# Two small touch loads (44 packets in all) ahead of the first full loads of an attention and gMLP kernel

## The chip, the cores and the metric

One core of a Trainium2 chip runs the whole program. The metric is device time in microseconds (us); lower is better. A run's time is some 1.2 us longer than the span that a profile shows of it. A granted TensorE clock that is halved for a few microseconds shows as a mean clock of 0.998 instead of 1.0.

## The reference, cut to what matters

```python
h = x + _A_ref(_layernorm(x), wq, wk, wv, wo, beta)       # 32 heads, 4 segments of 512 rows, with a memory
return h + _B_ref(_layernorm(h), w_in, w_sp, b_sp, w_out) # gated MLP
```

x is 2048 x 1024 in bf16, and wv is 1024 x 1024 (2 MB). The first thing that TensorE can do is v = layernorm(x) @ wv for the first 512 rows. It needs x by chunks of 128 rows and wv by blocks of 128 rows. Such a block of wv (256 KB) is called a wv row below.

## The kernel before

Every operation is recorded by a helper and then put in order for each engine by a static scheduler; the order of TensorE is fixed by the program. All loads are issued by SyncE. Start of the program, with cuts (the comments on the right are added here):

```python
N_WARM = 11
LOAD = "1 0:1 1:3 2 3:4 4:5 3 5:6 6:8"          # x chunk 1, wv row 0, wv rows 1-2, x chunk 2, ...
START = ("t00 t01 u00 u01 v00 u02 v01 T10 T11 v02 u03 v03 u10 ...")   # TensorE's order
...
ZERO = tens("zero", [128, L], BF16, R_E + 2048)
for k in range(N_WARM):
    mm(PS[:, 7, :], ZERO[:, 0:128], ZERO[:], True, True)
...
for h in range(2):
    x_cols(0, h)                                 # x chunk 0, two halves
for c in LOAD.split():
    if ":" in c:
        wv_rows(*map(int, c.split(":")))
    else:
        dma(XIN[int(c)][:], x2d[int(c) * 128:int(c) * 128 + 128, :])
act(G1[:, 0:1], ZERO[:, 0:1], ACTF.Sqrt)         # loads the first activation table
```

In START, t and T are transposes of a chunk of x. u and v are the two halves of the wv product, with the chunk as the first digit and the wv row as the second. So u01 is the first matmul that needs "1:3", the 512 KB load of wv rows 1 and 2. The text calls it the critical load; the prediction writes "wv rows 1 to 3" for it, after the slice.

The softmax here doesn't subtract the row's maximum and nothing guards it: scores larger than these inputs give would overflow.

Of the kernel before, what the change touches and what calls it, by code (L numbers as in the profile page):

```python
# [7 lines left out]
BF16 = mybir.dt.bfloat16  # L8
# [18 lines left out]
PE, ACT, DVE, POOL, SP = range(5)  # L27
# [319 lines left out]
def bass_sequential_preLN__memory_aug_infini_attn__mixer_gmlp__prompt_kernel(  # L347
# [14 lines left out]
    x2d = A_x[0]  # L362
# [9 lines left out]
    def region(size):  # L372
        a = cur[0]
        cur[0] += (size + 31) // 32 * 32
        assert cur[0] <= ARENA, cur[0]
        return a

    def tens(name, shape, dt, off=None):
        sz = int(np.prod(shape[1:])) * mybir.dt.size(dt)
        if off is None:  # L380
            off = region(sz)
        assert off % 32 == 0 and off + sz <= ARENA, (name, off, sz)
        t = nc.alloc_sbuf_tensor_at(name, list(shape), dt, offset=abase + off)
        G.base[t.name] = off
        return t
# [15 lines left out]
    R_E = region(20480)  # L401
# [52 lines left out]
    def n_of(ap):  # L454
        return int(np.prod([x[1] for x in list(ap.ap)[1:]]))

    def inps(ap):
        return ap.tensor.name == PS.name
# [15 lines left out]
    def act(o, i, func, scale=1.0, prio=0, bias=None):  # L474
        r = [i] + [x for x in (scale, bias) if x is not None and not isinstance(x, float)]
        kw = {} if bias is None else {"bias": bias}
        G.op(ACT, lambda e: e.activation(o, i, func, scale=scale, **kw), r, [o],  # L477
             ((172 if inps(i) else 224) + n_of(i)) / 1.2 + 26, prio=prio, name=str(func))
# [39 lines left out]
    def dma(o, i, transpose=False, after=False, eng=SP):  # L518
        nb = n_of(o) * list(o.ap)[0][1] * mybir.dt.size(o.dtype)
        d = G.op(eng, lambda e: e.dma_start(o, i, transpose=transpose), [i], [o], 1230.0 if transpose else 400.0, dma=True,  # L520
             nbytes=nb * (2.1 if transpose else 0.92 if n_of(o) == D or o.tensor.name == WV.name else 1.0), name=("T:" if transpose else "D:") + o.tensor.name)
        if after:
            d.deps.add(G.last_pe)
# [4 lines left out]
    def bank():  # L528
        b = bank_set[0][bank_rr[0] % len(bank_set[0])]
        bank_rr[0] += 1  # L530
        return PS[:, b, :]
# [9 lines left out]
    def wv_rows(a, b):  # L541
        dma(WV[:, a:b, :], A_wv.rearrange("(c p) n -> p c n", p=128)[:, a:b, :])
# [7 lines left out]
    for c in LOAD.split():  # L550
        if ":" in c:
            wv_rows(*map(int, c.split(":")))
        else:
            dma(XIN[int(c)][:], x2d[int(c) * 128:int(c) * 128 + 128, :])
    act(G1[:, 0:1], ZERO[:, 0:1], ACTF.Sqrt)
    iot = tens("iot", [128, 128], I32, R_E)
    G.op(POOL, lambda e: e.iota(iot[:], [[1, 128]], base=0, channel_multiplier=-1), [], [iot[:]], 400)
# [264 lines left out]
    for x in START.split():  # L822
        c, i = int(x[1]), int(x[2])
# [5 lines left out]
        b = PS[:, 2 + 2 * (c % 3) + h, :]  # L829
# [12 lines left out]
    for lo, hi in ((0, 128), (128, 512)):  # L842
        b = bank()
# [83 lines left out]
    for pair in range(16):  # L927
        a, b = 2 * pair, 2 * pair + 1
# [213 lines left out]
```

## Time and profile before

| | before |
|---|---|
| median of 3 runs | 794.76 us (794.14 to 795.21) |
| the profiled run | 796.87 us, span 795.6, mean clock 0.998 |
| critical load, issue to landing | 5.92 us, landed at 8.57 |
| start of u01 | 8.61 us |

### The profile page before, as it was taken

What the parts mean: (1) busy time and instruction counts of PE and PEld (TensorE: products, weight loads), DVE (VectorE), ACT (ScalarE), POOL (GpSimd) and SP (SyncE); (2) the same over time, 40 slices, a digit from 0 to 9 for tenths busy, and PEclk for the clock granted to TensorE, in tenths of its full rate; (3) what the DMA queues carried; (4) which work ended last, traced back from release to release, by engine and by line L of the source; (5) the groups of instructions that cost most, each with busy time, mean ns of one, the idle gap of its engine ahead of it and who ended that gap; (6) DMA issues with size and microseconds to landing.
All of it is one profiled execution on the core that took longest, in us unless ns stands there. A gap on an engine that the chain in (4) does not pass through costs nothing.

```text
span 795.6 us, 12064 instructions
## 1 busy us (share of the span) xinstructions
PE 790.3 (99%) x5369; PEld 321.2 (40%) x4760; DVE 369.9 (46%) x854; ACT 293.0 (37%) x351; POOL 138.8 (17%) x269
## 2 busy tenths in 40 slices
PE   8999999999999999999999999999999999999999
PEld 2455554555554542341322414443244334424433
DVE  6784687878775686804215042132233222322222
ACT  5788887787768862133323323100000000000000
POOL 1354544444433331200001010000000000000000
PEclk9999999999999999999999999999999999999999
DMA  7676812742234648510000016703410530012001
GB/s 245 179 167 140 173 42 67 138 90 55 68 75 112 159 115 228 159 42 1 0 1 1 20 34 148 202 1 64 121 34 1 119 100 1 0 54 61 0 1 53
DMA packets 128550, 65.02 MB, mean 82 GB/s; under 512 B 96624, under 2 KB 119408, under 8 KB 128496
## 3 DMA queue, kind: packets, MB, share of 16 engines
q1 hardware_dynamic: 128496, 64.25, 33.2%
q8 instruction: 39, 0.64, 0.4%
q14 instruction: 15, 0.12, 0.1%
HBM read 32.51 MB, written 8.39 MB: 51 GB/s over the span
## 4 chain that ended last, share of the span: by engine, by line
PE 98%; DMA 1%; ACT 0%; SPq 0%; issue 0%; DVE 0%
PE ps L327 80%; PE ps L328 15%; PE ps L468 3%; DMA wv<-in_A_wv_dram 1%; ACT e L477 0%; SPq L520 0%; PE ps L472 0%; DVE hx L499 0%
## 5 line engine op out<-in xcount | busy, mean ns | idle before, releaser
L327 PE MATMUL ps<-wspT,z 128*128 128x512 bf16 x896 | 194.0, 379 | 0.0
L477 ACT ACTIVATE e<-ps 128x2048 bf16<-128x2048 f32 x80 | 149.8, 1873 | 35.1 <-PE ps L468 35.1
L327 PEld LDWEIGHTS ps<-wspT,z 128*128 128x128 bf16 x896 | 87.7, 98 | 106.4 <-issue 1.0
L477 ACT ACTIVATE z<-ps 128x512 bf16<-128x512 f32 x120 | 63.1, 571 | 145.4 <-PE ps L327 145.4
L499 DVE TENSOR_TENSOR tg<-ps,brow 128x512 bf16<-128x512 f32 x56 | 38.7, 691 | 150.0 <-PE ps L327 122.0
L327 PE MATMUL ps<-hnT,win 128*128 128x512 bf16 x448 | 97.3, 379 | 0.0
L718 POOL TENSOR_SCALAR_AFFINE_SELECT e<-e 128x1024 bf16<-128x1024 bf16 (+1 forms) x80 | 77.1, 963 | 113.9 <-ACT e L477 113.6
L328 PE MATMUL ps<-win,hnT 128*128 128x512 bf16 (+1 forms) x384 | 90.1, 344 | 0.0
L327 PE MATMUL ps<-wout,y 128*128 128x512 bf16 (+2 forms) x252 | 85.8, 367 | 0.0
L572 DVE BATCH_NORM_STATS2 stats<-z 128x6 f32<-128x448 bf16 x64 | 40.1, 627 | 97.0 <-ACT z L477 95.4
L328 PE MATMUL ps<-wout,y 128*128 128x512 bf16 x210 | 79.6, 379 | 0.0
L499 DVE TENSOR_TENSOR hx<-hx,ps 128x512 bf16<-128x512 bf16 (+1 forms) x65 | 42.3, 675 | 77.3 <-PE ps L327 76.9
L327 PEld LDWEIGHTS ps<-hnT,win 128*128 128x128 bf16 x448 | 43.8, 98 | 54.2 <-issue 2.0
L327 PE MATMUL ps<-wv,xnT 128*128 128x512 bf16 x251 | 60.7, 384 | 1.6 <-DMA wv<-in_A_wv_dram 1.1
L327 PE MATMUL ps<-xnT,wk 128*128 128x512 bf16 (+2 forms) x264 | 60.8, 374 | 0.0
L327 PE MATMUL ps<-xnT,wq 128*128 128x512 bf16 x256 | 60.8, 380 | 0.0
L327 PE MATMUL ps<-wo,oT 128*128 128x512 bf16 x256 | 58.8, 379 | 0.0
L327 PEld LDWEIGHTS ps<-wout,y 128*128 128x128 bf16 x252 | 24.2, 98 | 72.2 <-issue 69.1
L327 PE MATMUL ps<-win,hnT 128*128 128x512 bf16 x128 | 48.5, 379 | 0.0
L327 PEld LDWEIGHTS ps<-win,hnT 128*128 128x128 bf16 x128 | 12.5, 98 | 81.4 <-issue 80.9
L513 POOL TENSOR_SCALAR rs<-mv 128x1 f32<-128x1 f32 x44 | 11.0, 250 | 194.2 <-DVE mv L575 194.2
L327 PEld LDWEIGHTS ps<-v,e 128*128 128x128 bf16 x1280 | 40.1, 96 | 9.8 <-issue 1.7
(76 smaller groups left out, 640.0 us busy)
## 6 DMA issues: line engine op xcount, KB each, us to landing
win<-in_B_w_in_dram SPq DMA_DIRECT2D x6, 1024.0 KB, 5.8
hx<-in_A_x_dram SPq DMA_DIRECT2D x16, 256.0 KB, 3.3
out_dram<-hx SPq DMA_DIRECT2D x16, 256.0 KB, 2.4
hx<-out_dram SPq DMA_DIRECT2D x16, 256.0 KB, 2.7
out_dram<-hx SPq DMA_DIRECT2D x31, 128.0 KB, 1.7
xin<-in_A_x_dram SPq DMA_DIRECT2D x15, 256.0 KB, 4.9
wout<-in_B_w_out_dram SPq DMA_DIRECT2D x2, 1792.0 KB, 11.0
wq<-in_A_wq_dram SPq DMA_DIRECT2D x2, 1024.0 KB, 7.9
```

Of the source, the lines that this page charges most:

```text
L327: return e.matmul(out, lhsT, rhs, start=start, stop=stop)
L328: return e.add_instruction(mybir.InstMatmult(name="I-%d" % (1000000 + o.idx), engine=e.engine, ins=[e.lower_ap(rhs), e.lower_ap(lhsT)], ou ...
L468: G.op(PE, lambda e: e.matmul(o, lhsT, rhs, start=True, stop=True, tile_position=(32 * i, 0)), [lhsT, rhs], [o], n / 2.4 if last else 3.5, ...
L477: G.op(ACT, lambda e: e.activation(o, i, func, scale=scale, **kw), r, [o], ((172 if inps(i) else 224) + n_of(i)) / 1.2 + 26, prio=prio, na ...
L499: G.op(DVE, lambda e: e.tensor_tensor(o, a, b, op), [a, b], [o], vcost(o, [a, b], fast), name="tt", prio=late[0])
L513: G.op(POOL, lambda e: e.tensor_single_scalar(o, i, s, op), [i], [o], 220 if n_of(o) < 8 else 220 + 2.5 * n_of(o), name="pts1", prio=late[0])
L572: G.op(DVE, lambda e, si=si, so=so: e.bn_stats(so, si), [si], [so], (cs + 143) / 0.96, name="bn_stats", prio=late[0])
L718: G.op(POOL, lambda e: e.affine_select(d, d, pat, ALU.is_ge, 0.0, base=0, channel_multiplier=-1), [d], [d], 1270 if j else 640, name="mask")
```

## The change

The intent: if the first read of each 64 KB piece of memory costs extra, a tiny read of every piece ahead of the full loads should pay for it early. The two touches go through ScalarE's queue, so that they delay none of SyncE's issues.

```diff
+    touch = [tens("touch%d" % i, [32, 32], BF16, R_E + 4096 + 64 * i) for i in range(2)]
+    dma(touch[0][:], A_wv.rearrange("(a b) n -> a b n", b=32)[:, 0, 0:32], eng=ACT)
+    dma(touch[1][0:12, :], x2d[128:512, :].rearrange("(a b) n -> a b n", b=32)[:, 0, 0:32], eng=ACT)
     act(G1[:, 0:1], ZERO[:, 0:1], ACTF.Sqrt)
```

## The prediction

> **What bounds the kernel now.** I read the page first: the busy shares, the slices, the chain that ended last. Then, because the change touches only the first loads, I read the first 26 us: the chain of waits in that stretch, TensorE's timeline, and a table by windows.
>
> ```profile
> PE 790.3 (99%) x5369; PEld 321.2 (40%) x4760; DVE 369.9 (46%) x854; ACT 293.0 (37%) x351; POOL 138.8 (17%) x269
> ...
> PE 98%; DMA 1%; ACT 0%; SPq 0%; issue 0%; DVE 0%
> ```
>
> TensorE carries 98% of the chain, and DMA 1%. The share of "busy" alone would prove little; the list of TensorE's waits says more. It has only five entries, 3.4 us in all, and all but 0.2 us lie before 8.6 us. So the change can gain in one place only, the start. The chain of waits between 0 and 28 us, in order of time (start, length, what):
>
> ```profile
> 2.61 0.04 issue
> 2.65 5.92 DMA wv<-in_A_wv_dram
> 8.57 0.05 issue
> 8.61 1.89 PE ps L327 x4
> 10.50 0.85 PE ps L472 x8
> 11.35 0.71 PE ps L327 x2
> ```
>
> One transfer, the 512 KB load of wv rows 1 to 3, takes 5.92 us from its issue to landing. It releases TensorE at 8.61 us, and from there TensorE sets its own pace to the end. TensorE's timeline shows the wait (start, length, engine, then what its idle time ended with):
>
> ```profile
> 5.96 0.62 PE L472 MATMUL ps<-ident,xin 128*128 128x128 bf16 x8 [0.35 <-DVE xin L493]
> 7.14 0.39 PE L327 MATMUL ps<-wv,xnT 128*128 128x512 bf16 x1 [0.57 <-ACT xnT L477]
> 8.61 1.89 PE L327 MATMUL ps<-wv,xnT 128*128 128x512 bf16 x4 [1.08 <-DMA wv<-in_A_wv_dram]
> 10.29 1.06 PE L472 MATMUL ps<-ident,xin 128*128 128x128 bf16 x8
> ```
>
> Four matmuls from 8.61 to 10.29 us are 0.42 us each; later ones follow each other every 0.216 us. The clock column of the table by windows (length, TensorE busy, granted clock, DMA share, GB/s) tells why; I cut the windows where the record of the clock changes:
>
> ```profile
> 0.00:4.97 4.97, 3.73 (x9) 0.10 (x1) 3.49 (x5) 1.63 (x3) 2.02 (x13) 1.00 0.46 134
> 4.97:8.38 3.41, 1.65 (x12) 0.54 (x9) 2.63 (x7) 2.74 (x8) 0.00 (x0) 1.00 1.00 332
> 8.38:11.79 3.41, 3.18 (x14) 1.57 (x14) 1.52 (x4) 1.54 (x4) 0.00 (x0) 0.50 1.05 401
> 11.79:15.20 3.41, 3.41 (x20) 1.64 (x19) 2.21 (x8) 2.02 (x6) 0.00 (x0) 1.00 0.94 298
> ```
>
> After a window in which TensorE was busy 1.65 of 3.41 us, the clock is halved for 3.41 us. The late load thus costs twice: its wait, and possibly the half clock after it.
>
> The same loads seen from the DMA side, by microsecond (window, length, TensorE busy, clock, DMA share, GB/s):
>
> ```profile
> 3.00:4.00 1.00, 1.00 (x4) 1.00 0.55 127
> 4.00:5.00 1.00, 1.00 (x3) 1.00 0.92 295
> 5.00:6.00 1.00, 0.65 (x4) 1.00 1.00 303
> ...
> 7.00:8.00 1.00, 0.39 (x1) 1.00 1.07 324
> ...
> 9.00:10.00 1.00, 1.00 (x4) 0.50 1.07 414
> ```
>
> The same stream reaches 414 GB/s at 9 us but 127 at 3 us. The trace's packet records give the reason: an ordinary 2 KB packet takes 75 to 84 ns, but about 17 between 3.0 and 3.5 us take 150 to 540 ns, two at 4.6 us take 1241 ns, two at 5.0 us take 1760 and 1820 ns, and another 17 between 7.4 and 7.9 us take 150 to 610 ns. None after 8.0 us and before 14 us takes over 132 ns, though those loads, too, read addresses for the first time. The 16 completion signals of the critical load come between 6.73 and 8.57 us: 14 within 0.72 us, the last two 1.72 and 1.84 us after the first. The same lag of two engines is in every later load of the start.
>
> **What the Trainium skill says.** "DMA: Bandwidth & Descriptors", section "Why a DMA increments its semaphore by 16 and not by 1": only the full count means that all data landed, so one late engine holds the load. The two late signals agree. Same page, section "Issuing engines are not separate DMA queues": loads issued by ScalarE run on the same 16 engines and interleave, so the touches are no free channel. No trace of before shows ScalarE's queue. "TensorE: Matmul & The Clock Gate", Part 1: the clock follows activity in a free-running window of 3413 ns; the 3.41 us windows agree, and the phase should vary from run to run. No page that I found says that a first read of a 64 KB piece of memory costs extra; that is the premise of the change, not a known fact.
>
> **The change part by part.** It removes nothing. It adds two DMA issues ahead of ScalarE's first activation. wv is 2 MB, so 32 reads of 64 bytes; x chunks 1 to 3 are 768 KB, so 12 reads: 44 packets, 2.8 KB, against 3 MB of full loads, nothing in bandwidth. Issue cost: a plain load costs SyncE 0.43 us, so 2 x 0.43 = 0.86 us on ScalarE. ScalarE's first activation ends at 2.28 us and its next is due at 4.83 us after 2.55 us of idling, so even at 3.14 us nothing is late. The destination is scratch in the region of the exponentials, first written after 26 us: no wait.
>
> What could be gained: the touches are issued near 0.8 and 1.2 us, the first wv load at 2.18 us and x chunk 1 at 1.7 us. If the slow packets are a cost per 64 KB piece that a prior read pays, wv gains a lead of 1 us. Then the last two signals of the critical load vanish: it lands at 6.73 + 0.72 = 7.45 us, 1.12 us earlier. Four matmuls then run at full clock from 7.45 to 8.35 us instead of 8.61 to 10.29 us, and the transposes of chunk 1 can start at 8.35 us (their input is ready when VectorE ends at 7.78 + 0.55 = 8.33 us): 10.29 - 8.35 = 1.9 us gained. Later loads would not take this back: wv row 3 (landing at 9.93 us now, used at 11.57), x chunk 2 (normalised at 13.13, used at 14.92), the first half of wk (landing at 22.83, used at 24.65): slack of 1.6, 1.8 and 1.8 us, and the first two come earlier as well. If TensorE's activity also keeps the clock up, at most 3.41 / 2 = 1.7 us more, most of it then eaten by the loads, which arrive no faster than 414 GB/s. Sum where it works: 1.5 to 2.2 us, thus about 793 us.
>
> **The rivals.** (1) No effect: the slow packets are not a matter of 64 KB pieces. For it: the long ones are only four packets, and slow ones are absent from wv rows 4 to 8, and packets of wk at 18 us show 200 to 540 ns when the engines had stood idle, which looks like a queue starting up. Then 794.8 us, within the noise of 0.5 us. (2) The touches pay the stall, but on the engines and at the time at which x chunk 0 comes: it lands at 3.11 and 3.53 us and leads to the first transposes at 5.96 us. A stall of 1.2 to 1.8 us there would push TensorE's start past 8.61 us (slack: the first matmul was ready at 7.14): up to 0.7 us worse. (3) The touch comes too late: the full reads arrive while the touch's own is still under way, and gain a part, 0.3 to 1 us. (4) The clock's phase moves by chance: either way up to 1.7 us in single runs, smaller in the median; before spread 1.1 us.
>
> **Range and chances.** I give the working case 0.4 at 793.0, no effect 0.4 at 794.7, harm 0.2 at 795.2: mean 0.4 x 793.0 + 0.4 x 794.7 + 0.2 x 795.2 = 794.1. The range, 792.4 to 795.5 us, spans the working case with a little help from the clock and the harmful one with noise. 2% is 16 us, more than the whole start could give: within 2% is all but certain.
>
> **What would show it.** Works: the critical load lands near 7.5 us, no packet of over 1 us before 8 us, TensorE's second stretch of wv matmuls starts near 7.5. No effect: landing at 8.3 to 8.8 us and the same two late signals. Harm: x chunk 0 lands after 3.6 us, first transposes after 6.3. I would be wrong in the sum if the start moved by 2 us and the end did not, that is, if a later wait (wk, chunk 4 of x near 33 us) took it back, or if the schedule, recomputed with two more operations, reordered work elsewhere.

## The result, and the profile after

| | before | after |
|---|---|---|
| median of 6 runs | 794.71 us | 794.79 us |
| range | 794.14 to 795.21 | 794.23 to 795.21 |

The six runs of before are the three above and three more. The ratio of after to before is 1.0001, with an interval of 0.9988 to 1.0013. Ratios here are the mean time of one kernel's runs over the mean of the other's of the same rounds, so not quite the ratio of the medians. No change is visible.

The two profiles, however, differ by 2.6 us: that of before is the slow draw above, that of after is of the fastest of its six runs (794.23 us). The chain of waits of the changed kernel up to 10 us (start, length, what), to be held against the chain that the prediction shows:

```profile
1.85 4.27 PE ps L328 x10
6.11 0.49 PE ps L472 x4
6.61 0.02 issue
6.63 0.61 ACT xnT L477
7.24 0.04 issue
7.28 1.25 PE ps L327 x5
8.54 0.52 PE ps L472 x8
```

No DMA stands on it: the critical load landed at 6.99 us, before TensorE asked for it. In the table by windows, the third window (8.38 to 11.79) now has a clock of 1.00, where the prediction's table has 0.50 (length, then busy time of TensorE, its weight loads, VectorE, ScalarE, GpSimd, then clock, DMA share, GB/s):

```profile
4.97:8.38 3.41, 2.94 (x16) 1.04 (x13) 2.63 (x8) 3.09 (x9) 0.00 (x0) 1.00 0.99 360
8.38:11.79 3.41, 3.41 (x23) 1.72 (x22) 2.83 (x8) 2.98 (x9) 0.00 (x0) 1.00 1.06 398
```

Read alone, this pair of profiles says that the touches work as hoped. The timed runs say that they do nothing. To see which part of the program the 2.6 us belong to, look at the first logits matmul (L468) in TensorE's timeline, before and then after:

```profile
26.49 0.39 PE L468 MATMUL ps<-qk 32*128 32x512 bf16 x4
```

```profile
23.91 0.39 PE L468 MATMUL ps<-qk 32*128 32x512 bf16 x4
```

From there to the end, before takes 795.6 - 26.49 = 769.1 us and after takes 793.0 - 23.91 = 769.1 us. The same subtraction gives 769.1 us in all 14 profiles. So the rest of the program neither takes back nor adds anything: a microsecond gained or lost at the start is one gained or lost in the end. The 2.6 us of difference are 1.10 us by which u01 starts later (8.61 against 7.51) and 1.5 us more from u01 to the logits (17.9 against 16.4), about what a half clock over 3.41 us can cost (at most 1.7).

### The profile page after: what moved, and what is told of

Same layout as the page of the kernel before. It is cut to its first block, busy times and chain, and to the rows that moved or that the text cites. A ratio compares the mean times of both kernels' runs of the same rounds, so it can differ in the third digit from the quotient of the medians. Undisturbed runs are those within 1.5% of the kernel's fastest.

```text
span 793.0 us, 12068 instructions
## 1 busy us (share of the span) xinstructions
PE 789.3 (100%) x5369; PEld 320.6 (40%) x4760; DVE 369.9 (47%) x854; ACT 293.1 (37%) x351; POOL 138.8 (18%) x269
## 4 chain that ended last, share of the span: by engine, by line
PE 99%; ACT 0%; DVE 0%; issue 0%
PE ps L327 81%; PE ps L328 15%; PE ps L468 3%; ACT e L477 0%; PE ps L472 0%; ACT xnT L477 0%; DVE hx L499 0%; DVE zero L535 0%
```

## The experiments

**Theories.** CHANCE: the touches change nothing, and the two profiles are two draws from one distribution. TOUCH: they do bring the critical load earlier, and something in the timed runs hides it.

### Control, repeat and decoy

The control is the kernel before, unchanged, and the repeat is the changed kernel, unchanged. The decoy keeps both small loads, their shapes and their queue, but reads elsewhere:

```diff
-    dma(touch[0][:], A_wv.rearrange(...
-    dma(touch[1][0:12, :], x2d[128:512, :].rearrange(...
+    dma(touch[0][:], A_wo.rearrange(...
+    dma(touch[1][0:12, :], x2d[1536:1920, :].rearrange(...
```

> The kernel before, unchanged, as a control. Theory CHANCE (the touches do nothing; the profile of before was a slow draw): the time ratio is 1.000 within 0.1%, the profiled span is 793 to 794 us, the critical load of wv rows 1 to 3 lands before 8 us, and no half-clock window appears, all without any touch. Theory TOUCH (the touches do bring the load earlier, 8.57 to 6.99 us): the load lands at 8.3 to 8.8 us again, with two engines 1.7 us late, and the span is 795 to 796 us.

> The changed kernel again. CHANCE: ratio 1.000 within 0.1%, landing anywhere from 7.0 to 8.6 us, slow packets of over 0.9 us as before. TOUCH: landing at 6.9 to 7.3 us again, and a ratio below 1 by 0.1% or more (0.9980 to 0.9990).

> Same two small loads in ScalarE's queue, same shapes, but they read wo and x chunks 12 to 14, which no early load needs. CHANCE: same time as the changed kernel within 0.1%, and the same number of slow packets (over 0.14 us) before 8 us, some 40 to 50. TOUCH: landing back at 8.3 to 8.8 us, time 1.5 to 2.5 us above the changed kernel.

The median of five runs was 794.75 us for the control, 794.74 for the repeat and 794.71 for the decoy; the ratios to before were 1.0005, 1.0001 and 1.0000, with intervals of about 0.13% either way. The line of the critical load in the chain of waits (issue, time to landing), first the control, then the repeat, then the decoy:

```profile
2.65 5.34 DMA wv<-in_A_wv_dram
7.99 0.05 issue
8.04 1.04 PE ps L327 x4
```

```profile
2.65 5.38 DMA wv<-in_A_wv_dram
8.03 0.05 issue
8.07 1.04 PE ps L327 x4
```

```profile
2.64 5.19 DMA wv<-in_A_wv_dram
```

The kernel without touches lands the load at 7.99 us, the one with touches at 8.03, and the one with useless touches at 7.83. The four matmuls after it take 1.04 us where the prediction's profile has 1.89: in these runs the clock was full. TOUCH had the control at 8.3 to 8.8 us with a span of 795 to 796, and the repeat at 6.9 to 7.3; both missed (the control's span is 793.5). The landing at 6.99 us did not come again. Over all batches, the 17 runs of the changed kernel average 794.70 us and the 28 full-clock runs of the kernel before (those whose clock is listed) 794.69.

The slow packets did not become fewer either. Loads of the first 14 us had this many packets over 0.14 us: 49, 43 and 49 in the three profiles of the kernel before (the third is below), 50, 54 and 43 in the three of the changed kernel, and 55 with the decoy (CHANCE had some 40 to 50). A usual packet of 2 KB takes 0.08 us.

One of the control's five runs took 796.73 us with a clock of 0.998, close to the profiled run of before (796.87, also 0.998), without any change in the program.

### Full loads held back until the touches have landed

A touch beside the loads could be too late to help. So every load after x chunk 0 was made to wait for both touches:

```diff
+    led = [len(G.ops) - 2, len(G.ops) - 1]       # the two touches, now recorded first
     for c in LOAD.split():
         ...
+        G.ops[-1].deps.update(led)
```

> The touches as in the change, but every load after x chunk 0 is issued only when both touches have landed (about 3.2 us instead of 1.7 us). CHANCE: slow packets appear all the same in the loads that follow; everything at the start comes 1.0 to 1.6 us later and the time rises by about as much (795.7 to 796.3 us). TOUCH (it needs a lead): no packet over 0.3 us in x chunk 1 and wv, the load takes under 4.5 us from issue to landing, and the time is at most 0.3 us above before.

It took 800.72 us, far more than either theory had. The edit was faulty: the load of half of wq carries no such wait, so the scheduler put that 1 MB ahead of x chunk 1 and wv. The critical load then landed at 11.54 us, and the clock was halved twice as long (0.996). The run says nothing on the touches. One detail is of use: the packets of x and wv, which now came after 1 MB of other traffic, had hardly any slow ones (three of its 2 KB packets took over 0.14 us in the first 14 us).

The mended version holds wq and betab too, so the order of issue is that of before. A second one does the same with the decoy's addresses:

```diff
     w_half(WQ, A_wq, 0)
+    G.ops[-1].deps.update(led)
     dma(BETAB[:], A_beta.partition_broadcast(128))
+    G.ops[-1].deps.update(led)
```

> The hold of the first attempt, mended: x chunk 1, wv, x chunks 2 and 3, wq and betab are all issued, in the order of before, once both touches (of wv and x) have landed, about 3.2 us. PIECES (a first read of each 64 KB piece is what costs, and a touch pays it): at most 5 packets over 0.3 us in x chunk 1 and wv, and the 512 KB load takes 4.0 us or less from issue to landing. START-UP (the slow packets come with the first burst on the 16 engines, whatever the addresses): 15 or more packets over 0.3 us, 5 us or more from issue to landing. Either way 1.5 us later at the start: 795.7 to 797.5 us, the half clock included.

> The same hold, but the two small loads read wo and x chunks 12 to 14, so wv and x chunk 1 are untouched when their loads start. PIECES: 15 or more packets over 0.3 us and 5 us or more for the 512 KB load, against the run with real touches. START-UP: the same count and the same time as that run, within the scatter of single profiles (a third).

The times were 797.82 and 797.77 us (ratios to before 1.0031 and 1.0034), a little above the 795.7 to 797.5 expected. The chain of waits with real touches, then with decoys:

```profile
1.24 2.11 DMA touch<-in_A_x_dram
...
4.22 5.83 DMA wv<-in_A_wv_dram
```

```profile
1.24 1.96 DMA touch<-in_A_x_dram
...
4.06 5.67 DMA wv<-in_A_wv_dram
```

With its pieces touched 1 us and more before the first packet, the critical load took 5.83 us from issue; with untouched pieces it took 5.67. Packets over 0.3 us in the first 14 us: 40 with real touches (35 of them in the 2 KB packets that were held back), 13 with decoys, the wrong way round for the premise. A difference of two single profiles proves little by itself, but the premise asked for at most 5 in the first. START-UP, which asked for the same count in both within a third, missed there too. The small prior read of each 64 KB piece, as built here, does not make the later read faster: the two profiles and the equal times show it.

Two readings of the kept traces go further. The 44 touch packets, which were the first reads of their pieces in the program, took 8 to 11 ns each in every profile that has them, so no such cost shows in their records. And the kernel reads x a second time, for the residual sum. Chunk 2, read in full at the start, is read again by a load of the same shape, issued at 106.26 us in the profile of before: 16 of its 128 packets took over 0.14 us, the longest 0.61, and 10 to 22 did in the other five profiles of the two kernels. So slow packets need no first read. (Whether a touch and the later full read ran on the same DMA engine isn't in the records, and whether a piece that was read long ago costs again was not tested.)

What does make these packets slow is not shown. At the start they come in the first 6 to 9 us of the main burst, with touches or without and whenever it starts, which fits START-UP but is not an explanation.

### What an earlier critical load would be worth

First attempt: the critical load goes to scratch, and GpSimd fills the wv rows 0 to 2 on chip.

```diff
-        dma(WV[:, a:b, :], ...
+        dma((SCR if b <= 3 else WV)[:, a:b, :], ...
+    G.op(POOL, lambda e: e.memset(WV[:, 0:3, :], 0.01), [], [WV[:, 0:3, :]], 2900, name="memset")
```

> Wrong result on purpose: the loads of wv rows 0 and 1 to 2 go to scratch, unused, and GpSimd fills those rows of wv on chip, so TensorE no longer waits for the critical load; the transfers stay. This is the most that any help to that load could give. TensorE goes on at 7.2 to 7.5 us instead of 7.9 to 8.1 us (fast draws) or 8.6 (slow): 0.5 to 0.8 us less than before, 793.9 to 794.2 us. If the prediction's sum was right (1.5 to 2.2 us to be had from the typical run), below 793.2 us.

It was no faster: 796.35 us (794.68 to 798.24), ratio 1.0013, interval 0.9996 to 1.0030; two of its six runs had the half clock, and one took 798.24 us without it. In its profile, wv row 3 landed at 10.68 us and became the wait, where the profiles of before have it at 9.33 to 9.93. Whether the 2.69 us memset, which runs beside the first loads, disturbs them, or the scratch address does, stays open. The edit changed more than the wait, so a cleaner one followed: the first 64 matmuls read the zero tile, and nothing else is touched.

```diff
-        mm(b[:], XNT[0][:, i, c * 128:(c + 1) * 128], WV[:, i, 512 * h:512 * h + 512], i == 0, i == 7)
+        mm(b[:], XNT[0][:, i, c * 128:(c + 1) * 128], ZERO[:], i == 0, i == 7)
```

> Wrong result on purpose: the first 64 wv matmuls read the tile of zeros in place of wv, so TensorE waits for no wv load; every transfer stays as it is. The most that faster wv loads alone could give. If the typical wait for the critical load (0.6 to 0.8 us after TensorE is ready at 7.2 us) is the only loss: 0.4 to 0.8 us less, 793.9 to 794.3 us, and no half-clock runs. If the prediction's 1.5 to 2.2 us was right for a typical run: 792.5 to 793.2 us.

The median was 794.64 us (794.23 to 794.72), ratio 0.9989 with an interval of 0.9974 to 1.0004. The control in the same batch had 794.40, the changed kernel 794.64. So with no wait for wv at all, the typical run is no faster that can be seen, and both forecasts missed. The means of the version and of the control differ by 0.04 us, give or take 0.4 (95%, worked out from their five and six runs): a gain of 1.5 us is excluded, one of 0.4 is not. The chain of waits of its profile shows what can take the place:

```profile
1.71 3.85 DMA xin<-in_A_x_dram
5.56 0.02 issue
5.58 0.62 ACT hx L591 x2
6.21 0.02 issue
6.23 0.71 ACT hx L593 x2
6.94 0.49 ACT xnT L477
7.43 0.05 issue
7.47 1.25 PE ps L327 x5
```

x chunk 1, which landed at 5.56 us (4.54 to 5.36 in the seven profiles of the two kernels and the decoy, so this draw is a late one), holds up ScalarE's sums over it (L591, L593). The first evacuation of transposes (xnT: ScalarE copies TensorE's result to where TensorE can read it), which TensorE waits for, stands behind them in ScalarE's order. TensorE goes on at 7.47 us. Its next transposes, those of chunk 1, start at 8.56 us, and in the control of the same batch at 9.19 (TensorE's timeline, first without the wait, then the control):

```profile
8.56 0.61 PE L472 MATMUL ps<-ident,xin 128*128 128x128 bf16 x8
```

```profile
9.19 0.61 PE L472 MATMUL ps<-ident,xin 128*128 128x128 bf16 x8
```

Its logits begin at 24.03 us against 24.38 and 24.66 in the two controls: 0.3 to 0.6 us, within the spread of single draws.

The opposite: 512 KB of other data ahead of the critical load.

```diff
+            if c == "1:3":
+                dma(SCR[:], A_wo.rearrange("(c p) n -> p c n", p=128)[:, 0:2, :])
             wv_rows(*map(int, c.split(":")))
```

> A load of 512 KB of wo into scratch ahead of the critical load, which delays it and all later ones by an estimated 1.3 us (512 KB at 400 GB/s). If the start chain passes on to the end one for one: 1.3 us more, 796.0 us, or 797.5 to 797.8 with a half-clock window in most runs (clock column 0.998). If the start has slack: no change from 794.7 us.

It took 798.17 us, ratio 1.0036, a little above the 797.5 to 797.8 forecast, and all six runs had the clock of 0.998. The load landed at 9.64 us, 1.4 to 1.7 us later than in the controls. Its windows around the change of clock:

```profile
7.40:10.81 3.41, 1.52 (x10) 0.75 (x11) 1.18 (x3) 1.16 (x3) 0.00 (x0) 1.00 1.02 378
10.81:14.22 3.41, 3.41 (x15) 1.33 (x12) 2.72 (x8) 2.82 (x10) 0.00 (x0) 0.50 1.06 382
```

After a window with TensorE busy for 1.52 us, the clock is halved. The window just before this one, 3.98 to 7.39 us, had 1.76 us and was not followed by a half clock. The 3.3 us above the median of before (794.92) are about the delay (some 1.5 us) and the half clock (1.7 us, half of 3.41): a late load does cost twice, as the prediction had it. It is the typical run that has little of it to win.

### The half clock

> The kernel before again, for its profile and for the share of half-clock runs (clock column 0.998): so far 1 of 14 runs on one chip and 3 of 11 on another. CHANCE: the same share as the changed kernel in this batch, within what five runs can show, and the critical load landing between 7.0 and 8.6 us.

> The changed kernel again, on the same chip as the control. CHANCE: runs split as those of before do: 794.2 to 795.7 us at full clock, 796.5 to 797.7 us with a half-clock window, and load landing between 7.0 and 8.6 us. A rival of its own, GUARD: the touches leave typical runs alone but prevent the half-clock window; then none of its five runs shows 0.998 where before shows two or more of its runs here.

Control: 794.40 us (794.04 to 795.02), ratio to the other runs of the same kernel 0.9988; an identical kernel differs by 0.12%, which is what these ratios are good for (the runs of before that they divide by include three with the half clock). Changed: 794.64 us (794.15 to 794.90), ratio 0.9990. Their critical loads landed at 8.27 and 8.06 us:

```profile
2.64 5.63 DMA wv<-in_A_wv_dram
```

```profile
2.65 5.41 DMA wv<-in_A_wv_dram
```

The clock of 0.998 was in no run of either in this batch. Over all batches, the kernel before had it in 4 of the 32 timed runs whose clock is listed (796.61 to 797.67 us; all others 794.04 to 795.72), besides its profiled run. The changed kernel had it in none of 17. If its share were one in eight too, 17 runs without would come up in (7/8)^17 = 10% of such trials. So GUARD is neither shown nor refuted for the kernel as it stands. It can't be a power of the touches as such, for the held-back version has them and was halved in 4 of 4 runs.

> Three idle matmuls on zeros, two while TensorE waits for the first evacuation and one while it waits for the critical load. If the half clock comes from too little activity in one window (1.65 us of 3.41 was halved[...]), the added 0.65 us keep every run at full clock: none at 0.998, all runs 794.2 to 795.7 us, median within 0.3 us of before. If the half clock has another cause, its share stays as in the control.

```diff
+        for _ in range({"u00": 2, "u01": 1}.get(x, 0)):
+            mm(PS[:, 7, :], ZERO[:, 0:128], ZERO[:], True, True)
```

None of six runs was halved, but neither was any of the control's, so this tells nothing on the guard. And it was slower: 795.77 us (795.26 to 796.50), each of its six runs above all six of the control. (Its ratio of 1.0006, interval 0.9992 to 1.0020, has half-clock runs in the divisor.) The scheduler, given three more operations, placed the second table load ahead of an evacuation that TensorE needs. ScalarE's timeline:

```profile
12.59 1.28 ACT L837 ACT_TABLE_LOAD   x1
13.89 0.20 ACT L837 ACTIVATE g<-rs 128x1 f32<-128x1 f32 x1
13.99 0.58 ACT L477 ACTIVATE xnT<-ps 128x512 bf16<-128x512 bf16 x1
```

TensorE waits 0.35 us for that tile, until 14.63 us. The profile is of the fastest of the six runs, so this explains a part of the 1.4 us; the rest is not shown. The version is no use as built, and no version here is faster than the kernel before or the changed one.

## Why the prediction was right or wrong

The measured 794.79 us lies in the range of 792.4 to 795.5, and the class, within 2%, was all but certain. Neither speaks for the mechanism: the range was laid over the working case, no effect and harm alike, and the case that came true was one of two given 0.4. The steps beneath fared differently.

- **Only the start can gain: right.** The rest took 769.1 us in every profile.
- **The cost of the touches: right, and hidden.** ScalarE issued them in 0.42 and 0.64 us, 1.06 us against the 0.86 predicted. Its first activation then ended at 3.41 us, and the next was due at 4.88. The touches' packets took 0.01 us each, so nothing was lost in bandwidth.
- **"If the slow packets are a cost per 64 KB piece that a prior read pays": this failed.** It had a chance of 0.4. Landing was 6.99, 8.03 and 8.06 us with touches and 8.57, 7.99 and 8.27 without, with slow packets as many. Touching 1 us ahead gave 5.83 us from issue, not touching 5.67. The touches' own packets show no cost, and a second read of x has slow packets again. (The prediction's second group of "another 17" slow packets, between 7.4 and 7.9 us, counts 14 in the trace.) The first profile after, with its landing at 6.99, met every sign that the prediction had named for "works" except that four packets of over 1 us remained; two more draws took it away.
- **The sum of 1.5 to 2.2 us: mis-sized for the typical run.** It was read from a profile that was itself a slow draw (796.87 us, clock 0.998). The mis-sized term is the 10.29 us in 10.29 - 8.35 = 1.9, where the transposes of chunk 1 start: it holds the late landing and four matmuls at half clock. In the two controls they start at 8.91 and 9.19 us, so the same subtraction leaves 0.6 and 0.8 us. With every wait for wv removed they start at 8.56 us, not 8.35, because in that profile x chunk 1 and ScalarE's order hold TensorE until 7.47 us; a chain of waits of before could not show that wait, since the later arrival hides the earlier. What is left, 0.3 to 0.6 us, did not show in the times (794.64 us, control 794.40). (Between the two single profiles, slow draw against lucky one, the difference was 2.6 us, more than the sum.)
- **Rival 1, no effect: right**, at the 794.8 us given for it. The reason offered, a start of the queue rather than a matter of addresses, fits the held-back runs, but its mechanism stays open.
- **Rival 2, harm: not seen.** x chunk 0 landed at 3.16 and 3.56 us, against 3.11 and 3.53.
- **Rival 3, too late: refuted** by the held-back run. **Rival 4, the clock: right in kind.** It is not a spread within all runs, but a second group: one run in eight, 1.9 to 3.0 us above the median.

## What to carry to other kernels

Compare the time of the profiled run with the timed runs before taking a number from its profile: if it lies outside their range, its waits need not be those of the median. Two single profiles can differ by more than the effect sought, so profile the unchanged kernel again before believing a before-and-after pair. Find the worth of a wait by removing it (here, a zero tile in place of the weights) before spending effort on shortening it.

## What the Trainium skill lacked or had wrong

- "DMA: Bandwidth & Descriptors", section "Latency and other measured facts": nothing there on slow packets in the first burst of a program. In the 14 profiles here, 33 to 72 packets of the first 14 us took 0.14 to 1.85 us (a usual one of 2 KB takes 0.08), and a prior read of the same 64 KB pieces did not help.
- The same section gives some 600 ns to the first byte for loads issued from SyncE or ScalarE, but not the moment from which they count. In the changed kernel, the first packets of the first load began 0.62 us after its issue ended and 1.02 us after it started (issue 0.79 to 1.19 us, packets from 1.81); for the first touch it was 0.96 and 1.39 us (issue 0.78 to 1.21, packets from 2.17). Counted from the end of the issue, the first agrees and the second is longer.
- "TensorE: Matmul & The Clock Gate", Part 1, has the half clock follow an idle window of some 3.4 us, and does not say how much work keeps a window from counting as idle. Here it followed windows in which TensorE was busy for 1.65 us (before), 1.52 us (512 KB more), 1.06 and 0.85 us (held back) of 3.41, and did not follow ones with 1.76 us (512 KB more, the window before) and 1.91 us (second control). By the profile's count, a window that is nearly half busy still led to the half clock.
